# Delta-rule recurrence and top-1 experts on one core: products merged per head pair and per two batches, and expert tables read one expert ahead

## The chip, the core and the metric

The kernel runs on one core of a Trainium2 chip. A core has a matrix engine (TensorE; PE in the profile, its weight loads PEld), a vector engine (VectorE, DVE), a scalar engine (ScalarE, ACT), GpSimd (POOL), SyncE (SP), which here issues DMAs, and 16 DMA engines. Matrix products read their weights and their moving operand from SBUF and write into PSUM, which VectorE and ScalarE read. The metric is the device time of one execution in microseconds.

## The reference

Part one is a gated delta rule for 4 batches and 8 heads over 768 positions with heads of 48; part two sends each of the 3,072 rows to one of 8 experts (384 to 1,024 to 384).

```python
k_n = k / (norm(k) + 1e-6)
state = zeros(B, H, D, D)                       # B, H, S, D = 4, 8, 768, 48
for t in range(S):
    y[t]  = q[t] @ state
    v_old = k_n[t] @ state
    state = state + beta[t] * outer(k_n[t], v[t] - v_old)
x = y as (B*S, H*D)
logits = x @ w_gate
e = argmax(logits);  g = softmax(logits)[e]
out = g * (relu(x @ w1[e]) @ w2[e])             # per row, w1 384x1024, w2 1024x384
```

## The kernel before

**The recurrence in chunks.** The 768 positions are cut into 24 chunks of 32, and a block is four chunks. Partition 32b + s holds position s of a chunk of batch b. Within a chunk the rule is a triangular system: with G the products of keys with keys, u = inverse(I + scaled strict G) times (scaled v - k times state), then state += k'u and y = q times state + masked(q k')u. All products are fp32, and one fp32 matmul stands in the trace as two records of TensorE and two weight loads.

Heads go in pairs. Head 2p is on partitions 0 to 47 and head 2p + 1 on 64 to 111 of `kq_t` (keys and queries, transposed, by block), and the state `st_t` is [112, B, 4 pairs, 48] in the same way. TensorE is used in tiles: `tile_position` gives the row and column at which a small weight is put, so that small products of different tiles lie beside each other.

**One step t of the loop (one chunk), in TensorE's order:**
- `residual`, L288: key times state, 32 products with a 48 x 32 weight and 48 moving columns, into two PSUM tiles `ks`; VectorE subtracts each from v (L299, two instructions)
- `turn`, L360: three 128 x 128 transposes of the previous step's output row, for the logits; ScalarE copies them (L361, L362)
- `state_out`, L305: query times state, 32 products, into `yb`
- `dummy`, L467: 24 products of a row of zeros (bf16, 192 columns) into spare PSUM columns; nothing reads them
- `apply`, L316: the inverse `wt` times v, 32 products 32 x 32 by 48; ScalarE copies the result to `u` (L318, twice)
- `logits`, L368, of the previous step, and every second step the slots of the rows (L388 to L437; TensorE's part is L407 and L410)
- `update`, L328: keys times u, 32 products with 64 rows, into two PSUM tiles `S`; keys come from `kz_t`, which holds zeros where a row belongs to the other batch. ScalarE copies S to `st_t` (L332, twice)
- `inside`, L341: the masked query-key product `gk_t` times u, 32 products 32 x 32 by 48, into `yb`; ScalarE copies the row (L354)
- `gram`, L172, for the chunk nine ahead: keys times keys and queries, 32 products 48 x 32 by 64; ScalarE copies all of it to `gk_t` (L181), and VectorE masks the query part in SBUF one step before its use (L186, 256 elements a partition).

The order of every engine is written out by hand (`manual_schedule`). The inverse of the next block is a chain of 62 steps on VectorE (`lanes`, L259 and L266: multiply, subtract), with a square root on ScalarE at its front (L214) and transposes (L272); `beside(t, i)` puts `STEPS = (3, 3, 3, 2, 2, 2, 2)` of them, and as many slot operations, between the parts of step t. ScalarE also scales v (L281, eight instructions a step). Loads of `kq` for the block three ahead go out at t = 0, 4 and 8, on SP's queue. From t = 16 or so GpSimd and SP already fetch the first expert's rows, and from t = 20 its weights are split into a high and a low part (L473, L474).

**The experts.** Each has room for 448 rows. `find` (L508 to L518) reads a table `xi` of the rows' numbers from DRAM on SP's queue, `fetch` (L522) gathers the rows `xr` from DRAM with GpSimd, `tokens` transposes them on TensorE (L598 and L601 for the first expert, L791 and L792 later); `ffn` runs the two layers (L542, L552), each as three products of high and low parts, with `relu` on ScalarE and VectorE (L545, L546). While expert e runs its 12 places, `tokens` of expert e + 1 advances at the places in `TOK`, and the weights of e + 1 are loaded and split at those in `PC`.

**Before the loop** the first block's inverse runs on VectorE, nine Grams run on TensorE, and 16 and then 40 dummies stand among them.

Of the kernel before, what the change touches and what calls it, by code (L numbers as in the profile page):

```python
# [21 lines left out]
TB = 4  # L22
# [19 lines left out]
def deltanet_moe(ctx, tc, kq, kv, bl_in, w_gate, w1, w2, out):  # L42
# [14 lines left out]
    qmask = cp.tile([128, 32], F32, name="qmask")  # L57
# [25 lines left out]
    DU = 24  # L83
    TS = 5
    TOK = (0, 2, 6, 8, 9, 10)
    PC = (1, 3, 4, 6, 8, 9, 11)
    TOK0 = (0, 2, 6, 8, 9, 10)
# [18 lines left out]
    S_ = [pss.tile([128, 2, NP, D], F32, name=f"S{g}") for g in range(2)]  # L106
    ks_b = [pss.tile([128, 512], F32, name=f"ks{a}") for a in range(2)]
    ks_ = [x[:, 0:NP * D].rearrange("t (p e) -> t p e", p=NP) for x in ks_b]
    yb = pss.tile([128, 2, 512], F32, name="yb")
    y_ = yb[:, :, 0:NP * D].rearrange("t a (p e) -> t a p e", p=NP)  # L110
# [6 lines left out]
    gk_t = [home(j).tile([128, TB, H, 2, 32], F32, name=f"gk{j}") for j in range(4)]  # L117
    kz_t = [lp.tile([128, 2, DM], F32, name=f"kz{j}") for j in range(3)]
# [4 lines left out]
    st_t = lp.tile([128, B, NP, D], F32, name="st")  # L123
    tiles = {tb: {} for tb in range(NT)}

    def load_kq(tb, x, engs):
        for a in range(2):
            engs[a].dma_start(out=kq_t[tb % 4][64 * a:64 * a + D, x], in_=kq[tb, a, :, x])

    def load_kz(n):  # L130
        for b in range(B):
            r = slice(32 * b, 32 * b + 32)
            nc.sync.dma_start(out=kz_t[n % 3][r, b % 2], in_=kv[n, r, 0])

    def load_v(n):
        nc.sync.dma_start(out=v_t[n % 4].rearrange("p h d -> p (h d)"), in_=kv[n, :, 1])

    def constants():
# [3 lines left out]
                                pattern=[[1, 128]], channel_multiplier=-1)  # L142
        for b in range(B):
            r = slice(32 * b, 32 * b + 32)
            nc.gpsimd.tensor_copy(qmask[r], cmask[r, r])
# [15 lines left out]
    def kq_of(n, x, a, p, b):  # L161
        return kq_t[n // TB % 4][64 * a:64 * a + D, x, n % TB, p, b]

    def gram(n, psum, x0, x1):
        i = n % TB
        kt = kq_t[n // TB % 4]
        gv = psum[:, :, 0:256].rearrange("s a (p x t) -> s a p x t", p=NP, x=2)
# [9 lines left out]
    def gk_view(n, x0, x1):  # L177
        return gk_t[n // TB % 4][:, n % TB, :, x0:x1].rearrange("s (p a) x t -> s a p x t", a=2)
# [527 lines left out]
    for t in range(NN):  # L706
# [33 lines left out]
        if t + 1 < NN:  # L740
            mask_q(t + 1)
# [274 lines left out]
```

## Time and profile before

| | |
|---|---|
| time | 713.64 us, median of 3 runs (713.09 to 714.28) |
| the profiled execution | 716.45 us, its span 714.7 us |
| mean granted clock of TensorE | 0.849 of full speed |
| TensorE matmul records | 11,617, busy 550.7 us (77% of the span) |
| TensorE weight loads | 11,617, busy 495.9 us (69%) |
| VectorE | 1,273 instructions, 326.8 us (46%) |
| ScalarE | 626 instructions, 235.8 us (33%) |
| GpSimd | 132 instructions, 108.3 us (15%) |

The span is what the hardware profiler saw between the first and the last instruction; the 1.75 us by which the execution is longer lie around it. Busy times overlap between engines, and a matmul record's duration is longer than the distance to the next one where records are pipelined or run in different tiles, so the busy share of TensorE says little about how much of it could be saved. The granted clock has two levels in the records, 1.0 for 2.4 GHz and 0.5 for 1.2 GHz; a mean lies between them. An idle engine stands with what ended its wait; "issue" is time in which it waited for nothing that the profile shows.

### The profile page before, as it was taken

To read this page: it belongs to the slowest core of one execution; us is meant where nothing else is said; L and a number is where in the kernel's file an instruction comes from. 1 tells how busy PE (TensorE), PEld (TensorE's weight loads), DVE (VectorE), ACT (ScalarE), POOL (GpSimd) and SP (SyncE) were. 2 spreads that over 40 slices of the span, in tenths; PEclk is the share of its full clock that TensorE was granted. 3 is DMA by queue.
4 is the path that set the end of the run, shared out by engine and by line. 5 is a ranking of instruction groups with operands and counts; after the bars stand their busy time and mean duration, and the time that the engine had idled before them with its cause. 6 is when DMAs were issued, how large, how long until landed. Compare 5 with 4: busy or idle time off the path is not lost.

```text
span 714.7 us, 26302 instructions
## 1 busy us (share of the span) xinstructions
PE 550.7 (77%) x11617; PEld 495.9 (69%) x11617; DVE 326.8 (46%) x1273; ACT 235.8 (33%) x626; POOL 108.3 (15%) x132
## 2 busy tenths in 40 slices
PE   3253886586657767877877889799999999999991
PEld 3243775475556556766766789688988989898991
DVE  3937255364526366466443243363435363545311
ACT  1222232233224323333243243243434343434320
POOL 5000001010001101011012021331313222313111
PEclk9997787678768666779686789899999999999996
DMA  4867043605440530242234240463434353444000
GB/s 96 162 117 182 15 85 97 126 15 120 105 95 8 126 90 14 53 112 51 57 94 122 63 122 23 128 192 110 140 116 143 107 146 125 142 124 134 24 14 19
DMA packets 58037, 68.12 MB, mean 95 GB/s; under 512 B 30961, under 2 KB 50714, under 8 KB 56768
## 3 DMA queue, kind: packets, MB, share of 16 engines
q1 hardware_dynamic: 53056, 56.02, 31.2%
q0 software_dynamic: 4800, 10.00, 4.3%
q8 instruction: 91, 1.49, 1.0%
q10 hardware_dynamic: 64, 0.39, 0.2%
q14 instruction: 26, 0.21, 0.1%
HBM read 53.46 MB, written 13.02 MB: 93 GB/s over the span
## 4 chain that ended last, share of the span: by engine, by line
PE 57%; issue 19%; DMA 10%; ACT 6%; DVE 5%; POOL 2%; SPq 0%; POOLq 0%; DVEq 0%; ACTq 0%
PE y L552 12%; PE ks L467 11%; PE h L542 10%; DMA xr<-xn,xi 4%; PE gb L172 3%; PE S L328 3%; PE y L825 3%; PE ks L316 3%; ACT v L281 3%; PE yb L305 2%; PE ks L368 2%; PE yb L341 2%; DMA kq<-in_kq_dram 2%; PE ks L288 2%; DMA st_d<-idi,sli 2%
## 5 line engine op out<-in xcount | busy, mean ns | idle before, releaser
L467 PE MATMUL ks<-zrow 128*128 128x192 bf16 x608 | 92.4, 341 | 8.0 <-DVE v L299 6.1
L552 PE MATMUL y<-w2h,hx 128*128 128x384 f32 x352 | 96.2, 348 | 0.0
L467 PEld LDWEIGHTS <-zrow 128*128 128x128 bf16 x608 | 80.0, 137 | 16.2 <-issue 6.9
L444 POOL DMA_INDIRECT st_d<-idi,sli x24 | 25.9, 1080 | 361.4 <-DVE sli L437 225.3
L266 DVE TENSOR_TENSOR lw<-lw,tmp 128x84 f32<-128x84 f32 (+26 forms) x372 | 76.4, 248 | 0.0
L259 DVE TENSOR_TENSOR tmp<-lg,lw 128x84 f32<-128x84 f32 (+26 forms) x372 | 76.3, 247 | 0.0
L552 PEld LDWEIGHTS y<-w2h,hx 128*128 128x128 f32 x352 | 66.3, 195 | 0.9
L318 ACT COPY u<-ks 128x192 f32<-128x192 f32 x48 | 15.2, 318 | 150.7 <-PE ks L316 150.3
L172 PE MATMUL gb<-kq 48*32 48x64 f32 (+1 forms) x1664 | 27.5, 249 | 46.1 <-issue 28.8
L474 DVE TENSOR_TENSOR w2l<-w2r,w2h 128x768 fp32r<-128x768 f32 x32 | 30.9, 969 | 68.1 <-ACT w2h L473 67.8
L542 PE MATMUL h<-xl,w1h 128*128 128x448 f32 x168 | 61.6, 367 | 0.0
L542 PE MATMUL h<-xh,w1l 128*128 128x448 f32 x168 | 61.6, 367 | 0.0
L542 PE MATMUL h<-xh,w1h 128*128 128x448 f32 x168 | 61.4, 366 | 0.0
L552 PE MATMUL y<-w2l,hx 128*128 128x384 f32 x176 | 60.7, 345 | 0.0
L555 POOL DMA_INDIRECT out_dram<-yo,xi x32 | 31.4, 982 | 167.3 <-ACT yo L820 122.2
L172 PEld LDWEIGHTS gb<-kq 48*32 48x32 f32 x1664 | 21.3, 124 | 50.8 <-issue 36.1
L305 PE MATMUL yb<-st,kq 48*32 48x48 f32 x1472 | 24.6, 269 | 36.7 <-ACT xT L362 21.6
L305 PEld LDWEIGHTS yb<-st,kq 48*32 48x32 f32 x1472 | 19.3, 140 | 45.8 <-ACT xT L362 29.7
L522 POOL DMA_INDIRECT xr<-xn,xi x33 | 39.5, 1196 | 61.7 <-DMA xi<-st_d 54.4
L546 DVE SCALAR_TENSOR_TENSOR hx<-h,hx 128x448 fp32r<-128x448 f32 (+1 forms) x64 | 37.1, 584 | 22.9 <-ACT hx L545 22.5
L281 ACT ACTIVATE v<-v,nt_all 128x48 f32<-128x48 f32 x192 | 45.7, 325 | 0.0
L288 PE MATMUL ks<-st,kq 48*32 48x48 f32 x1472 | 29.7, 236 | 20.5 <-issue 18.0
(151 smaller groups left out, 925.2 us busy)
## 6 DMA issues: line engine op xcount, KB each, us to landing
w1r<-in_moe_w_dram SPq DMA_DIRECT2D x24, 512.0 KB
w2r<-in_moe_w_dram SPq DMA_DIRECT2D x32, 384.0 KB
kq<-in_kq_dram SPq DMA_DIRECT2D x23, 384.0 KB
v<-in_kv_dram SPq DMA_DIRECT2D x24, 192.0 KB
kz<-in_kv_dram SPq DMA_DIRECT2D x96, 48.0 KB
xn<-row SPq DMA_DIRECT2D x10, 394.0 KB
gd<-gk SPq DMA_DIRECT2D x20, 128.0 KB
lg<-gd SPq DMA_DIRECT2D x5, 512.0 KB
```

Source lines behind the costliest of these rows:

```text
L172: nc.tensor.matmul(gv[32 * b:32 * b + 32, a, p, x0:x1], lhsT=kt[r, 0, i, p, b], rhs=kt[r, x0:x1, i, p, b], start=True, stop=True, tile_pos ...
L259: nc.vector.tensor_tensor(out=x, in0=lg[:, r0:r1, c:c + 1].broadcast_to([128, r1 - r0, b - a]), in1=lw[:, c:c + 1, a:b].broadcast_to([128, ...
L266: nc.vector.tensor_tensor(out=lw[:, r0:r1, a:b], in0=lw[:, r0:r1, a:b], in1=x, op=ALU.subtract)
L281: nc.scalar.activation(out=vn[:, h], in_=vn[:, h], func=AF.Copy, scale=nt[:, h:h + 1])
L288: nc.tensor.matmul(dst[32 * b:32 * b + 32, p], lhsT=kq_of(n, x, a, p, b), rhs=st_t[64 * a:64 * a + D, b, p], start=(p == 0), stop=True, ti ...
L305: nc.tensor.matmul(y_[32 * b:32 * b + 32, a, p], lhsT=kq_of(n, 1, a, p, b), rhs=st_t[64 * a:64 * a + D, b, p], start=(p == 0), stop=True, ...
L467: nc.tensor.matmul(ks_b[1][:, 320:512], lhsT=busy[:, 0:128], rhs=busy[:, 0:192], start=True, stop=True, skip_group_check=True)
L522: nc.gpsimd.indirect_dma_start(out=XR[e][:, g], out_offset=None, in_=xn[0:128 * nt], in_offset=bass.IndirectOffsetOnAxis(ap=XI[e][:, g, 0: ...
L542: nc.tensor.matmul(ps, lhsT=w[:, d, fs], rhs=x_[:, d], start=(n == 0), stop=(n == len(terms) - 1))
L546: nc.vector.scalar_tensor_tensor(out=hl, in0=ps, scalar=0.0, in1=hh.bitcast(F32), op0=ALU.max, op1=ALU.subtract)
L552: nc.tensor.matmul(ps, lhsT=h(f)[h_], rhs=w2[w][:, f, :], start=(n == 0), stop=(n == len(terms) - 1))
L555: nc.gpsimd.indirect_dma_start(out=out, out_offset=bass.IndirectOffsetOnAxis(ap=idx, axis=0), in_=yo, in_offset=None, bounds_check=N - 1, ...
```

## The change

The order of the loop stays; most products get larger and fewer.

- **State per head pair.** `st_t` is block-diagonal, [112, B, 4, 96]: head 2p in rows 0 to 47 and columns 0 to 47, head 2p + 1 in rows 64 to 111 and columns 48 to 95, zeros elsewhere (set once, by GpSimd). `residual` and `state_out` are 16 products each, 112 x 32 by 96, into `kb` and `yb`, which hold 384 columns in a row. One subtraction and one copy of u, each of 384 elements, stand where two of 192 stood.
- **Update by batch rows.** Each batch has its own PSUM bank in `S`; 16 products use the 32 rows of one batch, 112 weight columns and 96 moving ones. `kn_t` is one load a chunk, padded to 112 columns per pair, in place of four into `kz_t`. Two ScalarE copies bring the diagonal blocks, 768 elements on 48 partitions each, into `st_t`.
- **Grams of two batches.** 16 products, 48 x 64 by 128, give the Grams of two batches with each other too. ScalarE copies the key part to `gk_t`; VectorE multiplies the query part with `qmask` (now 64 wide, zero outside each batch's own block) straight from PSUM into `gq_t` (12 buffers). The mask so stands with the Gram, nine chunks ahead of its use. `inside` is 16 products 64 x 64 by 48.
- **Dummies** are fp32, 128 x 128, and eight a step (`DU`) in place of 24; they stand before `state_out`. Before the loop they are 10 and 24 in place of 16 and 40.
- **`turn`** writes into `gb`, which the Gram leaves free, and is copied by one instruction.
- **Start.** The first block's key Grams are made by `gram0` into `gb`, and VectorE transposes them straight from PSUM. All nine Grams then follow, with five steps of the inverse between each Gram and its copy. A `kq` load covers 112 rows in one DMA.
- **Expert tables.** `find` runs one expert ahead: expert 1's table is read before expert 0's, from then on the table of e + 1 behind the gathers of e, with three buffers in place of two, and `TOK` has one place less.

```diff
-    DU = 24
+    DU = 8
...
-    TOK = (0, 2, 6, 8, 9, 10)
+    TOK = (0, 6, 8, 9, 10)
...
+    S_ = pss.tile([128, B, 512], F32, name="S")
+    sv = S_[:, :, 0:DM].rearrange("d b (p f) -> d b p f", p=NP)
+    kb = pss.tile([128, 512], F32, name="kb")
+    ks = kb[:, 0:DM]
+    yb = pss.tile([128, 512], F32, name="yb")
...
+    kn_t = [lp.tile([128, NP, 112], F32, name=f"kn{j}") for j in range(3)]
...
+    st_t = lp.tile([128, B, NP, 2 * D], F32, name="st")
...
+    def gram(n):
+        i, kt = n % TB, kq_t[n // TB % 4]
+        for p in range(NP):
+            for c in range(2):
+                for a in range(2):
+                    r, bs = slice(64 * a, 64 * a + D), slice(2 * c, 2 * c + 2)
+                    nc.tensor.matmul(gb[64 * c:64 * c + 64, a, 128 * p:128 * p + 128],
+                                     lhsT=kt[r, 0, i, p, bs].rearrange("d b t -> d (b t)"),
+                                     rhs=kt[r, :, i, p, bs].rearrange("d x b t -> d x (b t)"), start=True, stop=True,
+                                     tile_position=(64 * a, 64 * c), skip_group_check=True)
+
+    def gram_copy(n):
+        gv = gb.rearrange("s a (p x t) -> s p a x t", p=NP, x=2)
+        if n >= TB:
+            nc.scalar.copy(out=gk_t[n // TB % 2][:, n % TB].rearrange("s (p a) t -> s p a t", a=2), in_=gv[:, :, :, 0])
+        nc.vector.tensor_tensor(out=gq_t[n % GQ].rearrange("s (p a) t -> s p a t", a=2), in0=gv[:, :, :, 1],
+                                in1=qmask.unsqueeze(1).unsqueeze(1).broadcast_to([128, NP, 2, 64]), op=ALU.mult)
...
+    def from_state(x, n, dst):
         for p in range(NP):
             for b in range(B):
...
+                nc.tensor.matmul(dst[32 * b:32 * b + 32, 2 * D * p:2 * D * p + 2 * D], lhsT=kq_of(n, x, p, b),
+                                 rhs=st_t[0:112, b, p], start=(p == 0), stop=True, tile_position=(0, 32 * b),
+                                 skip_group_check=True)
...
     def residual(n):
...
+        from_state(0, n, kb)
+        nc.vector.tensor_tensor(out=vflat(n), in0=vflat(n), in1=ks, op=ALU.subtract)
...
+    def update(n):
+        kn, u = kn_t[n % 3], u_t[n % 2]
         for p in range(NP):
             for b in range(B):
...
+                r = slice(32 * b, 32 * b + 32)
+                nc.tensor.matmul(sv[0:112, b, p], lhsT=kn[r, p], rhs=u[r, 2 * p:2 * p + 2].rearrange("t a e -> t (a e)"),
+                                 start=(n == 0 and p == 0), stop=True, tile_position=(32 * b, 0), skip_group_check=True)
         for a in range(2):
...
+            r, c = slice(64 * a, 64 * a + D), slice(D * a, D * a + D)
+            nc.scalar.copy(out=st_t[r, :, :, c], in_=sv[r, :, :, c])
...
     def inside(n):
...
+        gq, u = gq_t[n % GQ], u_t[n % 2]
+        for h in range(H):
+            for c in range(2):
+                r = slice(64 * c, 64 * c + 64)
+                nc.tensor.matmul(yb[r, D * h:D * h + D], lhsT=gq[r, h], rhs=u[r, h], start=(n == 0 and h == 0), stop=True,
+                                 tile_position=(64 * c, 64 * c), skip_group_check=True)
...
     def dummy(k):
         for _ in range(k):
-            nc.tensor.matmul(ks_b[1][:, 320:512], lhsT=busy[:, 0:128], rhs=busy[:, 0:192], start=True, stop=True,
+            nc.tensor.matmul(yb[:, DM:512], lhsT=zrow[:, 0:128], rhs=zrow[:, 128:256], start=True, stop=True,
                              skip_group_check=True)
...
-            XI[e] = rp.tile([128, NG + 1, 2], I32, name=f"xi{e}", tag="xi", bufs=2)
+            XI[e] = rp.tile([128, NG + 1, 2], I32, name=f"xi{e}", tag="xi", bufs=3)
...
-    dummy(40)
+    dummy(24)
...
             turn(t - 1)
+            dummy(DU)
             state_out(t)
-            dummy(DU)
...
-            gv = gram(t + GA, gb, 0, 2)
-            gram_copy(t + GA, gv, 0, 2, nc.scalar.copy)
+            gram(t + GA)
+            gram_copy(t + GA)
...
-        if t + 1 < NN:
-            mask_q(t + 1)
...
     def tokens(e, X):
-        find(e, 0 if e > 0 else NG)
         if e == 0:
             X.extend(X0["x"])
-        yield
+            find(0, NG)
+            find(1)
+            yield
         fetch(e, 0 if e > 0 else NG)
+        if 0 < e < E - 1:
+            find(e + 1)
         yield
```

TensorE's order in a step of the loop, from `inside` to the dummies, before (numbers behind a name tell buffers apart; 24 pairs of the last two rows follow each other):

```order
L341 MATMUL yb<-u_130,gk_118 32x48 x32
L172 MATMUL gb<-kq_116 32x64 x32
L288 MATMUL ks_110<-st,kq_114 32x48 x16
L288 MATMUL ks_111<-st,kq_114 32x48 x16
L360 MATMUL yb<-ident,row_1013 128x128 x3
L305 MATMUL yb<-st,kq_114 32x48 x32
L467 LDWEIGHTS zrow
L467 MATMUL ks_111<-zrow 128x192
```

and after, up to the logits:

```order
L331 MATMUL yb<-u_138,gq_121 64x48 x16
L179 MATMUL gb<-kq_115 64x128 x16
L292 MATMUL kb<-st,kq_113 32x96 x16
L349 MATMUL gb<-ident,row_1618 128x128 x3
L455 MATMUL yb<-zrow 128x128 x8
L292 MATMUL yb<-st,kq_113 32x96 x16
L311 MATMUL kb<-v_135,wt_1469 32x48 x32
L356 MATMUL kb<-wg,xT_140 128x8 x3
```

Four groups of 32 products are now 16 (`inside` L331, Gram L179, residual and state_out L292), the eight dummies stand ahead of state_out, and the transposes L349 write into the Gram's tile `gb`.

VectorE's order with its semaphore waits, from a mask to the next subtraction, before (`lg`, `lw` and `tmp` belong to the inverse, 128 x n is the size):

```order
L186 TENSOR_TENSOR gk_118<-gk_118,qmask 128x8x32
L266 TENSOR_TENSOR lw_173<-lw_173,tmp_2_1018 128x14x3 [waits DVE_49]
L266 TENSOR_TENSOR lw_173<-lw_173,tmp_2_1018 128x15x3 [waits DVE_49]
...
L259 TENSOR_TENSOR tmp_5_1084<-lg_654,lw_173 128x78 [waits DVE_49]
L259 TENSOR_TENSOR tmp_5_1084<-lg_654,lw_173 128x78
L299 TENSOR_TENSOR v_126<-v_126,ks_110 128x4x48 [waits DMAHW6_49,PE_49,Activation_49]
L299 TENSOR_TENSOR v_126<-v_126,ks_111 128x4x48 [waits PE_49,Activation_49]
```

and after:

```order
L188 TENSOR_TENSOR gq_126<-gb,qmask 128x512 [waits Activation_49]
L263 TENSOR_TENSOR tmp_11_1024<-lg_615,lw_181 128x120 [waits DVE_49]
L263 TENSOR_TENSOR tmp_11_1024<-lg_615,lw_181 128x120
L270 TENSOR_TENSOR lw_181<-lw_181,tmp_11_1024 128x10x12 [waits DVE_49] x2
...
L270 TENSOR_TENSOR lw_181<-lw_181,tmp_13_1044 128x18x12 [waits DVE_49]
L270 TENSOR_TENSOR lw_181<-lw_181,tmp_13_1044 128x18x2 [waits DVE_49]
L301 TENSOR_TENSOR v_135<-v_135,kb 128x384 [waits DMAHW4_49,PE_49]
```

The mask stood at the same place and waited for no other engine; it now reads `gb` and waits for ScalarE, whose Gram copy comes just before it, and the inverse's steps and the subtraction stand behind it.

SP's queue at the last table reads ahead of the expert loop, before:

```order
L516 DMA xi_6810<-st_d 64x2 x2
L513 DMA xi_7991<-st_d 128x4
L518 DMA xi_7991<-st_d 128x2
L516 DMA xi_7991<-st_d 64x2 x2
L488 DMA w2r_0_8013<-in_moe_w_dram 128x2x384
```

and after:

```order
L504 DMA xi_4701<-st_d 64x2 x2
L501 DMA xi_5578<-st_d 128x4
L506 DMA xi_5578<-st_d 128x2
L504 DMA xi_5578<-st_d 64x2 x2
L501 DMA xi_5598<-st_d 128x4
L506 DMA xi_5598<-st_d 128x2
L504 DMA xi_5598<-st_d 64x2 x2
L476 DMA w2r_0_5620<-in_moe_w_dram 128x2x384
```

A second table, expert 2's, is read at the same place, ahead of a load of expert weights. GpSimd's order has not changed.

## Rows read from the trace of the kernel before

**Rows 1.** The page: busy time and share of the span of each engine with its instructions, and one row of its DMA queues (packets, MB, share of 16 engines).

```profile
PE 550.7 (77%) x11617; PEld 495.9 (69%) x11617; DVE 326.8 (46%) x1273; ACT 235.8 (33%) x626; POOL 108.3 (15%) x132
...
q8 instruction: 91, 1.49, 1.0%
```

**Rows 2.** Busy times of the loop and of the experts. Columns: start and end in us, length, busy us (and records) of PE, PEld, DVE, ACT and POOL, granted clock, DMA share, GB/s.

```profile
58.00:400.00 342.00, 246.61 (x8863) 213.97 (x8863) 169.80 (x885) 109.70 (x387) 24.03 (x23) 0.74 0.34 80
485.00:715.00 230.00, 209.30 (x1116) 197.16 (x1115) 91.83 (x150) 83.45 (x140) 52.52 (x54) 0.97 0.34 103
```

**Rows 3.** The chain of waits that ended last, in order of time: start in us, us, engine, what, line, records.

```profile
58.02 2.12 PE S L328 x44
...
189.64 1.43 PE ks L316 x64
...
253.70 4.00 PE ks L467 x24
...
384.03 1.15 PE S L328 x53
...
503.25 11.05 PE h L542 x54
```

**Rows 4.** What the engines waited for from 58 to 400 us, TensorE and VectorE: the waiting group, what ended the wait, total us, times, longest.

```profile
PE ks L288 <- issue: 18.0, 10, 2.9
PE gb L172 <- issue: 17.3, 8, 4.2
...
PE yb L305 <- issue: 15.0, 5, 5.4
...
PE S L328 <- issue: 5.3, 2, 3.7
...
DVE r L216 <- ACT s L214: 17.4, 5, 5.5
```

**Rows 5.** The DMA queues from 58 to 345 us, the row of TensorE's instructions.

```profile
q8 instruction: 58, 0.95, 1.6%
```

**Rows 6.** The timeline of some places: start in us, us, engine, line, what, tile, shapes, and in brackets the idle time before with what ended it.

```profile
239.38 0.88 PE L316 MATMUL ks<-v,wt 32*32 32x48 f32 x64
...
241.54 1.14 PE L328 MATMUL S<-u,kz 64*64 64x48 f32 x64
...
242.78 0.86 ACT L332 COPY st<-S 112x384 f32<-112x384 f32 x2 [0.96 <-PE S L328]
...
246.51 0.68 PE L172 MATMUL gb<-kq 48*32 48x64 f32 x32 [2.63 <-issue]
...
398.54 1.14 PE L328 MATMUL S<-u,kz 64*64 64x48 f32 x64
...
415.61 0.50 PE L542 MATMUL h<-xe,w1h 128*128 128x256 f32 x2 [0.70 <-DVE xe L474]
...
438.64 1.45 PE L598 MATMUL xt<-one,row 128*128 128x64 f32 x12
...
440.02 0.88 PE L601 MATMUL xt<-ident,xr 64*128 64x64 f32 x6
```

**Rows 7.** The table of Rows 2 for two applies.

```profile
189.70:191.00 1.30, 1.30 (x64) 1.19 (x63) 0.00 (x0) 0.32 (x1) 0.00 (x0) 0.50 0.00 0
239.40:240.20 0.80, 0.80 (x65) 0.73 (x65) 0.00 (x0) 0.21 (x1) 0.00 (x0) 1.00 0.93 373
```

**Rows 8.** Groups by line over the whole span: line, engine, operation, out<-in, shapes, count, busy us, mean ns of one, idle time before and what ended it.

```profile
L316 PE MATMUL ks<-v,wt 32*32 32x48 f32 x1536 | 25.3, 222 | 2.3 <-issue 2.3
...
L332 ACT COPY st<-S 112x384 f32<-112x384 f32 x46 | 19.7, 481 | 25.7 <-PE S L328 25.7
...
L318 ACT COPY u<-ks 128x192 f32<-128x192 f32 x48 | 15.2, 318 | 150.7 <-PE ks L316 150.3
...
L299 DVE TENSOR_TENSOR v<-v,ks 128x192 f32<-128x192 f32 x46 | 15.2, 351 | 27.0 <-PE ks L288 16.4 <-issue 10.4
...
L186 DVE TENSOR_TENSOR gk<-gk,qmask 128x256 f32<-128x256 f32 x24 | 10.0, 418 | 0.0
...
L546 DVE SCALAR_TENSOR_TENSOR hx<-h,hx 128x448 fp32r<-128x448 f32 (+1 forms) x64 | 37.1, 584 | 22.9 <-ACT hx L545 22.5
...
L427 DVE TENSOR_TENSOR pos<-pos,ohb 128x16 f32<-128x16 f32 (+1 forms) x14 | 2.4, 172 | 0.4
...
L542 PEld LDWEIGHTS h<-xh,w1h 128*128 128x128 f32 x168 | 31.6, 188 | 2.6
```

**Rows 9.** The timeline of VectorE in the first inverse: its first operation, the first of its 62 steps, and the transpose at its end.

```profile
14.50 0.19 DVE L210 TENSOR_SCALAR ss<-lg 128x32 f32<-128x32 f32 x1
...
18.47 0.25 DVE L259 TENSOR_TENSOR tmp<-lg,lw 128x15 f32<-128x15 f32 x2
...
39.28 1.96 DVE L272 STREAM_TRANSPOSE wt<-lw 128x1024 f32<-128x1024 f32 x1
```

**Rows 10.** Waits for gathered rows and their tables: TensorE from 470 us on, and GpSimd over the whole span.

```profile
PE xt L792 <- DMA xr<-xn,xi: 5.9, 6, 1.3
...
PE xt L791 <- DMA xr<-xn,xi: 1.7, 2, 1.3
...
POOL xr L522 <- DMA xi<-st_d: 54.4, 9, 9.6
```

More of the change, by code (lines that the diff above doesn't have):

```diff
@@ L301, in state_out, with apply @@
     def state_out(n):
+        from_state(1, n, yb)
+    def apply(n):
+        wt, vn, u = tiles[n // TB]["wt"], v_t[n % 4], u_t[n % 2]
+        for h in range(H):
+            for b in range(B):
+                r = slice(32 * b, 32 * b + 32)
+                nc.tensor.matmul(kb[r, D * h:D * h + D], lhsT=wt[r, n % TB * H + h], rhs=vn[r, h],
+                                 start=True, stop=True, tile_position=(32 * b, 32 * b), skip_group_check=True)
+        nc.scalar.copy(out=u.rearrange("t h e -> t (h e)"), in_=ks)
@@ L320, in update @@
-    def update(n):
-        kz, u = kz_t[n % 3], u_t[n % 2]
-        for s in range(2):
-            for p in range(NP):
-                for g in range(2):
-                    r = slice(64 * g, 64 * g + 64)
-                    for a in range(2):
-                        h, m = 2 * p + a, 64 if a == 0 else D
-                        nc.tensor.matmul(S_[g][64 * a:64 * a + m, s, p], lhsT=kz[r, s, h * D:h * D + m], rhs=u[r, h],
-                                         start=(n == 0 and s + p == 0), stop=True, tile_position=(64 * g, 64 * a),
-                                         skip_group_check=True)
-        for g in range(2):
-            nc.scalar.copy(out=st_t[0:112, 2 * g:2 * g + 2], in_=S_[g][0:112])
@@ L334, in inside @@
[L334 to L343 removed]
+                r = slice(32 * b, 32 * b + 32)
@@ L651, in deltanet_moe @@
     scale_v(1)
-    for n in range(TB, GA):
-        gv = gram(n, gb, 0, 2)
-        gram_copy(n, gv, 0, 2, nc.scalar.copy)
-        if n % TB == TB - 1:
+    for n in range(GA):
+        gram(n)
+        run(lane, 5)
+        gram_copy(n)
+        if n % TB == TB - 1 and n >= TB:
             grams_out(n // TB)
-    run(lane, 30)
-    mask_q(0)
-    run(lane, 20)
+    run(lane, 5)
     lw = tiles[0]["lw"]
-    nc.tensor.matmul(ks_b[1][0:32, 320:321], lhsT=lw[:, 10, 0:32], rhs=lw[:, 10, 0:1], start=True, stop=True,
+    nc.tensor.matmul(yb[0:32, DM:DM + 1], lhsT=lw[:, 10, 0:32], rhs=lw[:, 10, 0:1], start=True, stop=True,
                      skip_group_check=True)
-    dummy(40)
+    dummy(24)
     run(lane, 100)
@@ L843, in deltanet_moe @@
         for t in range(KF + NG + 1):
[L844 removed]
+            if e == 0 and t in (0, TS):
                 run(tok0)
```

154 lines of the change are left out of this document (52 added, 102 removed).

## The prediction, made before the changed kernel ran

> **What bounds the kernel now.** I read the stage table first. The recurrence, 58 to 400 us, takes 342 of the 714.7 us, the experts from 485 us on 230 [rows 2]. The chain of waits then gives the step: S L328, the state update, starts at 58.02 and, 21 updates later, at 384.03 [rows 3], 326.0 / 21 = 15.5 us a step. TensorE has 246.6 us of records there at a mean granted clock of 0.74, VectorE 169.8 us [rows 2]; neither fills the stretch. The waits say why: TensorE waits for "issue", 18.0 + 17.3 + 15.0 + 5.3 = 55.6 us in four rows [rows 4], and the timeline has one such wait inside a Gram, 2.63 us in front of its second half [rows 6]. The page gives the cause: TensorE's records are 11,617 matmuls and 11,617 weight loads, and queue q8 "instruction" carries 91 packets and 1.49 MB [rows 1]. That is 64 B a record and 256 records a packet. In this stretch TensorE executes 2 x 8,863 records [rows 2], 17,726 / 22 = 806 a step or 3.1 packets, and from 58 to 345 us 58 packets arrive [rows 5], one in 4.9 us. So the step is limited largely by how fast TensorE gets its instructions, and in part by a clock that is at 1.2 GHz half the time.
>
> **TensorE, part by part.** The 32 products of apply are 64 records in 0.88 us at a granted clock of 1.00 (2.4 GHz) and in 1.43 us at 0.50 (1.2 GHz) [rows 3, 6, 7]. Less the 0.22 us of the last record [rows 8], and with 16 records in each of its four tiles, that is 41 and 76 ns a record: about two cycles for each of 48 columns. Weight loads behave alike: 12 records with 128 weight columns and 64 moving ones take 440.02 - 438.64 = 1.38 us [rows 6], 115 ns each, again two cycles per column. So I price a product at (records per tile) x 2 x (the larger of moving and weight columns), tiles side by side, at full clock. Residual and state_out, four tiles: 8 x 192 cycles, 0.65 us each. Update, four tiles: 8 x 224, 0.8. Inside, two tiles: 16 x 128, 0.9. Gram, four tiles: 8 x 256, 0.9. Eight fp32 dummies: 16 x 115 ns, 1.85, where 24 bf16 ones took up to 4.00 [rows 3]. Apply, transposes and logits stay, 0.7, 0.4 and 0.7. No shape of the new tiles is in the trace. The lower bound for the new products is apply's 0.66 us / 63, 10.5 ns a record, or 0.35 us for 32; the upper one is that their tiles take turns (among the rivals). I take the tile price, since the 64x64 update of now, 1.14 us at full clock [rows 6], fits it: 16 records of 128 cycles are 0.85, plus the end of the last one.
>
> Records per step: 4 for each of 112 products (16 + 16 + 32 + 16 + 16 + 16), 6 for transposes, 12 for logits, 32 for dummies, about 4 for slots: 502 against 806, 2.0 packets instead of 3.1. At 4.9 us a packet that asks for 9.6 us a step.
>
> **The chain of a step after it.** ScalarE copies grow from 318 ns at 192 elements a partition to 481 at 384 [rows 8]: 0.85 ns an element. The state copies become two of 768 elements, 0.8 each, 1.5 us for both (now 0.86 [rows 6]; bounds 1.3 and 2.0). The mask now reads the Gram in PSUM, 512 elements: 0.67 us by the 584 ns of a PSUM operation of 448 [rows 8], with bounds of 0.42 (256 from SBUF) and 0.75. One subtraction of 384 takes 0.55 in place of two of 0.35 [rows 8].
>
> The mask is the new wait. What it waits for, the Gram copy, stands in ScalarE's order behind the state and row copies. Behind it on VectorE stand six steps of the inverse and the next subtraction, and the next step's transposes on TensorE wait for it too. From the end of an update: state copies until 1.6 us, row copy 2.05, Gram copy 2.65, mask 3.35, then six inverse steps of 0.33 (the first inverse: 39.28 - 18.47 less 0.42, over 62 steps [rows 9]) and some four slot operations of 0.17 [rows 8] until 6.0, subtraction 6.6, apply 7.5, u copy 8.05, update 9.05, with hand-overs 9.3. TensorE's own path (residual 1.8 to 2.7, transposes after the mask 3.8, dummies 5.7, state_out 6.4) lies just inside. VectorE's sum is nearly as long: one inverse, from its first operation at 14.50 to the end of its transpose at 41.24, is 26.3 us without the mask in it [rows 9], 6.6 a step over four steps; with subtraction 0.55, mask 0.67 and six slot operations a step, 8.8 us. On top comes ScalarE's square root, for which VectorE waits 17.4 / 5 = 3.5 us per inverse [rows 4], 0.8 us a step, and 0.1 for short packet waits: **10.2 us a step**. It is 9.3 if these hide, and 11.3 if short waits on both engines add up.
>
> Three steps load two blocks of kq, and TensorE's packets queue behind those loads; I keep 5 us for each, 15 in all, worked out from nothing better than the longest issue waits now.
>
> **The other stages.** Start to the first update, 58.0 us [rows 3]: the second kq load now starts behind a transpose of about 1.96 us [rows 9] and carries 112 rows instead of 96, and VectorE puts nine masks of 0.67 between the steps of the first inverse, where it had one of 0.42. The 24 fp32 dummies are 48 records, 5.5 us at full and 11 at half clock; they run beside the end of that inverse. Against it stand fewer Gram records (544 matmul records for 832) and eight small loads that became two. I come to 58 again, plus or minus 4. From the last update to the first early expert matmul, 398.54 to 415.61, 17.1 us [rows 6], there is one step and some hand-overs: 13. From there it is 299.1 us to the end, experts mostly. TensorE waits 5.9 + 1.7 = 7.6 us for xr in it, and GpSimd's gathers wait 54.4 us for tables [rows 10] that are now read one expert ahead. With the microseconds at half clock that follow the longest of these waits I take 9.5 (0 if another wait takes its place, 12 at most). No queue gains work there: on SP's queue the table reads move ahead of an expert's weight loads.
>
> **Sum**, against the profiled execution of 716.45 us: 1.75 around the span + 58 + 22 x 10.2 + 15 + 13 + 289.6 = 601.75. In general it is 377.4 + 22 P for a step of P us. The median of the runs shown, 713.64, lies 2.8 lower, so I predict **599 us**.
>
> **Rivals.** *Half clock* (0.14). At 1.2 GHz the step's products are 14.5 us of TensorE: residual and state_out 1.3 each, transposes 0.7, dummies 3.5, apply and logits 1.3 each, update, inside and Gram 1.7 each. For it: two applies, each right behind a burst of dummies, have 0.50 and 1.00 [rows 7], and the dummies become half as long. Against it: the idle stretches between bursts now are those of missing instructions. A step of 15 us half the time gives P = 12.2 and 646 - 2.8 = 643.
> *Instructions still bind* (0.10). The same data arrive in two thirds of the time, so a packet may need 6 us instead of 4.9: P = 11.8, 634.
> *The inverse hides better* (0.08). Mask and inverse steps overlap the rest: P = 9.0, 573.
> *Tiles take turns* (0.04), the slower side. Residual and state_out now use all rows and differ only in columns. If tiles that share rows work one after the other, each of 32 records costs 80 ns of stream and 27 of weights, 3.4 us instead of 0.65, and a Gram 16 records of 160 ns, 2.6: P about 16, 729 - 2.8 = 726. It decides from P = 15.4 on, where 377.4 + 22 P reaches 716.45. Against it: 54 expert matmuls, all on the same rows, take 11.05 us [rows 3], 205 ns each, while one load takes 188 ns [rows 8] and 448 columns at 2.4 GHz 187: load and stream overlap there.
> [...]
> That *the table read gains nothing* moves the sum by 9.5 us only and lies inside the range.
>
> **How the numbers follow.** The forecast (P from 9.3 to 11.3, 579 to 623) has 0.64. The range reaches to the half-clock case and to the one of 9.0 with a shorter start: 565 to 645. About 0.2% is what a measurement of this kernel can tell from no change; only the tiles' case and a hundredth of unknowns reach there: faster 0.95, same 0.01, slower 0.04.
>
> **What would show it.** About 63 instruction packets (502 records a step) and issue waits of TensorE under 25 us between first and last update; S starts some 10.2 us apart; the mask's wait for the Gram copy among VectorE's largest, and the subtraction on the chain; a granted clock over 0.9 there; residual near 0.65 + 0.2 us (2.6 or more would be the tiles' case); no wait for xr on TensorE from the third expert on. I am wrong if update starts lie over 12 us apart, or if the start grows by more than 6 us.

## The result and the profile after

The changed kernel takes 629.38 us (median of 4 runs, 620.08 to 632.35) against 713.96 of the kernel before: a ratio of 0.874, 95% interval 0.864 to 0.884. The ratio compares the means of the runs that lie within 1.5% of the fastest of their kernel (625.1 and 715.4 us), the others counting as slow; the two medians would give 0.882. The forecast was 599 us, with a range of 565 to 645. The profiled execution took 620.08 us with a span of 618.3.

The page of the changed kernel, its busy times and the queue that carries TensorE's instructions, as in [rows 1]:

```profile
PE 523.7 (85%) x7701; PEld 480.2 (78%) x7701; DVE 331.0 (54%) x1248; ACT 247.3 (40%) x572; POOL 102.0 (17%) x131
...
q8 instruction: 61, 1.00, 0.7%
```

Its table by stage, with the columns of [rows 2]: from the first update of the state to the last, from there to the first early expert matmul, and the rest.

```profile
55.74:309.69 253.95, 209.98 (x5297) 188.37 (x5297) 168.02 (x848) 120.78 (x340) 22.95 (x23) 0.89 0.42 114
309.69:327.68 17.99, 12.09 (x261) 10.42 (x260) 7.02 (x27) 7.42 (x17) 3.53 (x3) 0.85 0.30 77
327.68:618.28 290.60, 268.64 (x1468) 252.67 (x1468) 121.39 (x221) 110.07 (x190) 65.51 (x69) 0.95 0.35 109
```

The loop's 22 intervals now take 253.95 us, 11.5 each, where they took 340.5 [rows 3, 6]; the rest from the first early expert matmul went from 299.1 to 290.6 us. So 86.6 of the 96.4 us between the two profiled executions lie in the loop and 8.5 in the experts. TensorE's records there are 2 x 5,297 / 22 = 482 an interval. At a clock of 0.74 [rows 2] about 178 us of the loop stood at half clock before, at 0.89 about 56 us do now. How the 86.6 us divide between records, clock and waits, no run tells.

The two levels in the trace of the kernel before, by its dummies: those at 253.70 in [rows 3] took 4.00 us at a clock of 0.50, and at 1.00

```profile
336.34 2.14 PE ks L467 x24
```

So they follow each other, 192 columns each, in 158 and 82 ns, or 1.2 and 2.3 columns a nanosecond. The 1.2 and 2.4 GHz of the prediction stand for these two levels.

What the engines waited for from first to last update, as in [rows 4]:

```profile
PE gb L349 <- DVE gq L188: 8.5, 12, 1.0
PE kb L356 <- ACT u L313: 7.7, 13, 0.6
PE kb L311 <- DVE v L301: 6.4, 4, 2.0
PE kb L395 <- ACT u L313: 5.4, 9, 0.6
PE kb L356 <- DVE base L403: 4.8, 9, 0.5
PE kb L395 <- DVE ohb L390: 3.9, 1, 3.9
...
PE yb L331 <- issue: 1.4, 2, 1.0
```

```profile
DVE gq L188 <- ACT gk L187: 36.6, 15, 4.4
DVE w1l L462 <- ACT w1h L461: 13.2, 3, 9.7
```

The waits for "issue", 55.6 us of TensorE in [rows 4], are 1.4 us. A longer single wait that [rows 4] leaves out went with them, that of state_out for ScalarE's copy of the transposes:

```profile
PE yb L305 <- ACT xT L362: 21.0, 22, 1.9
```

The transposes wrote into `yb`, the tile of state_out; with `turn` in `gb` that wait is gone. The prediction has no term for it. What is left are short waits, for the mask (L349 are the transposes), for the copy of u (L356 are the logits, L395 the slots) and, four times, for the subtraction in front of apply (L311).

One step at full clock in the timeline of the changed kernel, from one update to the next; the columns are those of [rows 6]:

```profile
162.80 1.04 PE L320 MATMUL S<-u,kn 32*112 32x96 f32 x32
...
163.97 1.61 ACT L324 COPY st<-S 48x768 f32<-48x768 f32 x2 [0.89 <-PE S L320]
...
164.74 1.05 PE L179 MATMUL gb<-kq 48*64 48x128 f32 x30
...
165.73 0.87 PE L292 MATMUL kb<-st,kq 112*32 112x96 f32 x32
165.98 0.59 ACT L187 COPY gk<-gb 128x512 f32<-128x512 f32 x1
...
166.60 0.69 DVE L188 TENSOR_TENSOR gq<-gb,qmask 128x512 f32<-128x512 f32 x1 [2.02 <-ACT gk L187]
...
167.35 0.55 PE L349 MATMUL gb<-ident,row 128*128 128x128 f32 x3 [0.75 <-DVE gq L188]
...
167.73 1.95 PE L455 MATMUL yb<-zrow 128*128 128x128 f32 x16
...
169.61 0.87 PE L292 MATMUL yb<-st,kq 112*32 112x96 f32 x32
...
169.69 0.55 DVE L301 TENSOR_TENSOR v<-v,kb 128x384 f32<-128x384 f32 x1
...
170.41 0.88 PE L311 MATMUL kb<-v,wt 32*32 32x48 f32 x64
...
171.36 0.48 ACT L313 COPY u<-kb 128x384 f32<-128x384 f32 x1 [2.63 <-PE kb L311]
...
171.89 0.83 PE L356 MATMUL kb<-wg,xT 128*128 128x8 f32 x6 [0.60 <-ACT u L313]
...
172.66 1.04 PE L320 MATMUL S<-u,kn 32*112 32x96 f32 x32
```

The reader is to see that the step of 9.86 us follows TensorE's order: it stands for 0.75 us in front of the transposes, until Gram copy and mask are through, and 0.60 us in front of the logits, until u is copied, and else it works but for short gaps. The subtraction ends at 170.24 and apply starts at 170.41, when state_out is through: VectorE comes in just in time. With slot products in the step it is 10.84 us. Steps that lie partly at a clock of 0.50 take 11 to 14.

### The profile page after: what moved, and what is told of

Same layout as the page of the kernel before. It is cut to its first block, busy times and chain, and to the rows that moved or that the text cites. A ratio compares the mean times of both kernels' runs of the same rounds, so it can differ in the third digit from the quotient of the medians.

```text
span 618.3 us, 18249 instructions
## 1 busy us (share of the span) xinstructions
PE 523.7 (85%) x7701; PEld 480.2 (78%) x7701; DVE 331.0 (54%) x1248; ACT 247.3 (40%) x572; POOL 102.0 (17%) x131
## 4 chain that ended last, share of the span: by engine, by line
PE 66%; ACT 9%; DVE 9%; issue 7%; DMA 5%; POOL 1%; SPq 0%; POOLq 0%; ACTq 0%; DVEq 0%
PE h L530 17%; PE y L540 15%; PE yb L455 5%; PE gb L179 5%; PE S L320 4%; PE y L809 4%; ACT st L324 3%; PE kb L311 3%; PE kb L356 3%; PE yb L331 3%; DVE gq L188 2%; PE yb L292 2%; DMA kq<-in_kq_dram 2%; ACT u L313 2%; PE kb L292 2%
## 5 line engine op out<-in xcount | busy, mean ns | idle before, releaser
L540 PE MATMUL y<-w2h,hx 128*128 128x384 f32 x352 | 94.9, 344 | 0.0
L462 DVE TENSOR_TENSOR w2l<-w2r,w2h 128x768 fp32r<-128x768 f32 x32 | 30.9, 969 | 79.2 <-ACT w2h L461 78.6
L455 PE MATMUL yb<-zrow 128*128 128x128 f32 x436 | 61.7, 304 | 1.4 <-DVE warm L602 1.4
L455 PEld LDWEIGHTS yb<-zrow 128*128 128x128 f32 x436 | 60.1, 222 | 1.4 <-DVE warm L602 1.4
L179 PE MATMUL gb<-kq 48*64 48x128 f32 x768 | 41.3, 367 | 16.6 <-DVE gq L188 9.0
L533 ACT ACTIVATE hx<-h 128x448 fp32r<-128x448 f32 (+1 forms) x64 | 33.0, 517 | 45.7 <-PE h L530 45.7
L179 PEld LDWEIGHTS gb<-kq 48*64 48x64 f32 x768 | 33.1, 189 | 19.9 <-DVE gq L188 12.2
L324 ACT COPY st<-S 48x768 f32<-48x768 f32 x46 | 36.5, 793 | 23.6 <-PE S L320 23.0
L804 ACT ACTIVATE yo<-y,gt 128x384 f32<-128x384 f32 x22 | 12.8, 581 | 77.6 <-PE y L540 63.0
L313 ACT COPY u<-kb 128x384 f32<-128x384 f32 x24 | 11.5, 478 | 74.6 <-PE kb L311 64.7
L188 DVE TENSOR_TENSOR gq<-gb,qmask 128x512 f32<-128x512 f32 x24 | 16.6, 691 | 45.3 <-ACT gk L187 40.4
```

Source lines behind the costliest of these rows:

```text
L179: nc.tensor.matmul(gb[64 * c:64 * c + 64, a, 128 * p:128 * p + 128], lhsT=kt[r, 0, i, p, bs].rearrange("d b t -> d (b t)"), rhs=kt[r, :, i ...
L324: nc.scalar.copy(out=st_t[r, :, :, c], in_=sv[r, :, :, c])
L455: nc.tensor.matmul(yb[:, DM:512], lhsT=zrow[:, 0:128], rhs=zrow[:, 128:256], start=True, stop=True, skip_group_check=True)
L462: nc.vector.tensor_tensor(out=lo, in0=src, in1=hi.bitcast(F32), op=ALU.subtract)
L533: nc.scalar.activation(out=hh, in_=ps, func=AF.Relu)
L540: nc.tensor.matmul(ps, lhsT=h(f)[h_], rhs=w2[w][:, f, :], start=(n == 0), stop=(n == len(terms) - 1))
```

## The experiments

**The same kernel again, and records added.** The first run repeats the changed kernel for a second trace; the second puts tiny products behind the dummies:

```diff
             dummy(DU)
+            tiny(SM)            # SM = 152: bf16, weight 32 x 32, 8 columns, tiles in turn
```

> The changed kernel once more, for its spread and a second trace. Its times so far are 620.1 to 632.4 us. If the spread comes from the stretches at half clock in the loop, a trace with a longer time has more of them (57.8 us between first and last update in the first trace, where the loop took 253.9 us), while steps at full clock stay at 9.9 us, or 10.8 with slot products. If it comes from elsewhere (loads, experts), the loop is 254 us again and the difference lies behind 328 us.

> The changed kernel with 152 tiny products a step more (bf16, 32 x 32 by 8, four tiles, results not read), 304 records, so that a step has about 806 records as before the change. Theory of the prediction (delivery of TensorE's instructions limited the loop): about 3.1 packets a step at 4.9 us, steps of 15 us, TensorE's waits for issue back at 40 us or more in the loop, time about 700 us. Rival (work, not the number of records, set the step): only the products' own time is added, about 1 to 2 us a step, waits for issue stay under 15 us in the loop, time 645 to 665 us.

The repeat took 626.98 us (623.2 to 631.9); its profiled execution, 631.9 us, has the loop so:

```profile
55.40:322.04 266.64, 223.86 (x5296) 200.60 (x5296) 168.11 (x848) 121.12 (x340) 22.82 (x23) 0.82 0.39 109
```

The kernel before took 708.61 us beside it, a ratio of 0.885 (0.880 to 0.890). Against the first trace the loop is 12.7 us longer and the whole execution 11.8 us, so the difference between these two lies in the loop, where the clock is 0.82 for 0.89. With the two levels of 0.50 and 1.00, a stretch of length T at mean clock c has 2 (1 - c) T at half clock: 96 us against 56. Forty more microseconds at half clock go with 12.7 us of time, about 0.3 us each, and the 56 of the first trace are worth some 18 us. A step at full clock is 9.85 us again. Not all of the 12.7 need be the clock's: TensorE's waits for issue are 4.3 us here (2.6 in front of L331, 1.7 in front of L311).

With the added records the time is **737.31 us** (ratio 1.039 to the kernel before, 1.032 to 1.046), 110 us above the repeat. Its loop and its longest waits of TensorE there:

```profile
55.70:423.56 367.86, 297.64 (x8640) 268.99 (x8640) 168.40 (x848) 121.89 (x340) 22.83 (x23) 0.72 0.29 80
```

```profile
PE kb L312 <- issue: 18.6, 11, 2.8
PE yb L293 <- issue: 16.2, 7, 4.0
...
PE yb L458 <- issue: 5.5, 4, 1.6
```

```profile
L458 PE MATMUL yb<-zrow 32*32 32x8 bf16 x3344 | 30.8, 168 | 5.5 <-issue 5.5
```

The tiny products themselves are busy 30.8 us (L458), 1.4 a step. With 785 records a step the waits for issue are back at 41 us (these three and 0.7 more), the clock falls to 0.72, and the step is 16.7 us, longer than before the change. The rival, 645 to 665 us, falls: records with next to no arithmetic bring back the step of the kernel before, its waits and its clock. How the 110 us divide between missing instructions and the clock, beyond the 31 of work, the run doesn't tell, nor whether the clock fell behind the waits or behind the tiny products themselves.

That such waits are for instructions can be read in the traces of the two kernels. TensorE's 23,234 matmuls and weight loads before the change came in 91 packets of q8 [rows 1], 255 a packet. Counted in order by 256, all 29 waits for issue behind the first update in the loop before end within seven records of each other (179 to 185), and 1.2 to 1.7 us after a packet has come (the one in front of that update does not, at record 117 and 5.8 us); so do the two of the changed kernel, at 185 and 183, 1.4 and 1.5 us after one.

**Dummies.** `DU = 8` became 0 and 16.

> The changed kernel without the eight dummies of a step (nothing that is read is left out). Theory (in a step at full clock the dummies fill a gap in which TensorE would wait for VectorE's subtraction): such steps stay within 0.3 us of 9.9 and 10.8 us, the subtraction becomes the longest wait in front of apply (about 1.9 us each), and stretches at half clock grow from 57.8 us of the loop to 90 us or more: 625 to 650 us. Rival (the dummies lie on the path): steps at full clock shorten by 1.5 us or more, and the time falls below 610 us.

> The changed kernel with 16 dummies a step in place of eight. Theory (eight just fill the gap): a step at full clock grows by 1.7 to 1.9 us, 22 steps 40 us, and at most the 20 us that half clock costs now come back: 635 to 665 us, granted clock in the loop over 0.95. Rival (the clock is worth more than the gap): the time falls by 5 us or more, below 622 us.

Without dummies 625.98 us, the same as the repeat; with sixteen 652.86. Their loops:

```profile
55.25:316.92 261.67, 205.16 (x4944) 176.41 (x4944) 167.94 (x848) 121.82 (x340) 22.84 (x23) 0.72 0.40 110
```

```profile
56.80:343.08 286.28, 247.23 (x5648) 225.95 (x5648) 168.40 (x848) 120.68 (x340) 23.05 (x23) 0.90 0.36 101
```

And the waits for the subtraction without dummies:

```profile
PE kb L311 <- DVE v L301: 23.5, 16, 3.8
```

Sixteen go nearly as the theory had it: a first step of 11.64 us (updates at 56.83 and 68.47) is 1.8 more than with eight, 40 us in 22 steps, and the time is 26 us above the repeat. The clock is 0.90, about that of the first trace (0.89) and not the 0.95 expected. Without dummies both statements are half right: the first step at full clock is 8.85 us (updates at 55.26 and 64.11), so eight dummies do lengthen the path, by 1.0 of their 1.9 us; most of the rest is now waited for at the subtraction (0.72 us in this step). But half clock grows to 2 x 0.28 x 261.7 = 147 us, and the two cancel.

**Four suspects of a step.** The logits in another PSUM tile, `yb`; more of the inverse ahead of the mask; the mask ahead of the Gram copy (the two statements of `gram_copy` exchanged); and the tables read late again (`find(e)` in its old place, two buffers).

```diff
-        ps = kb[:, DM + E * (n % 2):DM + E * (n % 2) + E]
+        ps = yb[:, DM + E * (n % 2):DM + E * (n % 2) + E]
...
-            nc.tensor.matmul(yb[:, DM:512], lhsT=zrow[:, 0:128], rhs=zrow[:, 128:256], start=True, stop=True,
+            nc.tensor.matmul(yb[:, DM + 16:512], lhsT=zrow[:, 0:128], rhs=zrow[:, 128:240], start=True, stop=True,
```

```diff
-        inverses(STEPS[i], t)
+        inverses(ISTEPS[i], t)          # ISTEPS = (4, 4, 4, 4, 1, 0, 0)
```

> The changed kernel with the logits written to another PSUM bank (yb in place of kb, 16 columns that the dummies leave free), so that they need not wait until ScalarE has copied u out of kb. Theory (the logits' wait of 0.6 us stands on the path between apply and update in each step, and my sum left it and the 0.8 us of the logits out): steps at full clock become 9.2 to 9.4 us in place of 9.85, and 10.2 to 10.4 with slots in place of 10.84, loop 10 to 13 us shorter, time 612 to 618 us. Rival (VectorE has to finish an inverse in four steps, so what a step saves is waited for at the end of a block): ordinary steps shorten, but TensorE's waits for the subtraction grow from 5 to 10 us or more in the loop and the time stays at 622 to 630 us.

> The changed kernel with VectorE's steps of the inverse dealt out as 4, 4, 4, 4, 1, 0, 0 in place of 3, 3, 3, 2, 2, 2, 2: four more of them ahead of the mask, where VectorE waits for the Gram copy, and four fewer between the mask and the subtraction. Theory (that wait of 1.5 to 2 us a step is lost to the inverse, so that the subtraction stands late at the end of each block, TensorE idles 1.9 us there and the clock falls behind it): the waits of apply for VectorE at 97, 147 and 193 us go, DVE's waits for the Gram copy fall from 36.6 us to under 20 us, half clock in the loop falls under 45 us, time 605 to 618 us. Rival (the mask comes later in the steps with slots and holds up TensorE's transposes): TensorE's waits in front of the transposes grow from 8.5 us to 15 us or more, the time stays or rises, 625 to 640 us.

> The changed kernel with VectorE's mask ahead of ScalarE's Gram copy. Theory (TensorE's own path sets a step; the transposes wait for whoever reads the Gram last): mask and copy still follow each other, a step at full clock changes by no more than 0.3 us (9.85 to 9.6 at best), time 620 to 630 us. Rival (the mask's wait for the Gram copy is the new wait that sets the step, as the prediction had it): the mask starts 0.9 us earlier, steps at full clock become 9.0 to 9.2 us, time 605 to 613 us.

> The changed kernel with the expert tables read as before the change (one place ahead of their gathers, two buffers). Theory (7.6 us of waits for gathered rows and what half clock follows them): from the first early expert matmul to the end 298 to 300 us in place of 290.6, GpSimd waits 39 us or more for tables again, time 633 to 637 us. Rival (another wait stood behind them): 290 to 292 us from there on, time 622 to 629 us.

These four ran where the kernel before took 709.04 us, beside the repeat 708.61.

*Logits.* In this first form the first product of the logits carries the start flag in `yb`, between state_out and inside. By the author's reading the part of the output that comes from the state is so left out, and the rows go to other experts. It took 762.18 us, with TensorE waiting 143.4 us behind the experts for a gather that the other runs don't have, so only its loop is read: steps at full clock of 9.17 and 10.13 us, as the theory had it.

*The inverse earlier* gave 624.02 us, within the spread. VectorE's wait for the Gram copy fell from 36.6 to 32.6 us only, and neither the waits for the subtraction (4.2 us) nor the clock (0.86) changed as expected. The transposes waited 7.3 us, not more than before, so the rival falls too. Alone it does nothing that can be measured.

*The mask first* gave 627.71 us. A step at full clock stayed at 9.85 us (updates at 55.46 and 65.31) and one with slots went from 10.84 to 10.51 (updates at 78.50 and 89.01). Now the Gram copy waits for the mask, and the transposes for the copy, as long as before:

```profile
59.36 0.59 ACT L189 COPY gk<-gb 128x512 f32<-128x512 f32 x1 [0.63 <-DVE gq L186]
60.00 0.55 PE L349 MATMUL gb<-ident,row 128*128 128x128 f32 x3 [0.75 <-ACT gk L189]
```

So their order matters little. The run does not take the wait for the two away, and the 0.75 us stay on TensorE's path in either order.

*The tables late* gave 636.86 us, 9.9 above the repeat. From the first early expert matmul to the end:

```profile
335.22:633.80 298.58, 270.72 (x1468) 252.44 (x1468) 120.63 (x221) 108.57 (x190) 70.21 (x69) 0.96 0.34 106
```

```profile
POOL xr L510 <- DMA xi<-st_d: 32.6, 6, 7.0
```

298.6 for 290.6 us, and GpSimd waits 32.6 us for tables in this stretch (39 or more were expected), where no such wait is left in the changed kernel. TensorE waits 11.4 us for gathered rows in it, for 5.8.

**The logits again, and combined.** The same tile, now added without a start flag (`start=False`); then together with the inverse's steps as above and a block's two `kq` loads one step apart; then this with four dummies and with none.

```diff
-        if t % TB == 0 and 3 <= t // TB + 3 < NT:
-            for x in range(2):
-                load_kq(t // TB + 3, x, nc.sync)
+        if t % TB < 2 and t // TB + 3 < NT:
+            load_kq(t // TB + 3, t % TB, nc.sync)
```

> The logits in yb once more, now added without a start flag, so that the sum of the output in that bank is kept. Theory (the logits' wait of 0.6 us stood on TensorE's path in each step, and the stretch with this wait, the slots' wait of 0.5 us and products of 8 columns is where the clock fell): steps at full clock 9.2 us and 10.1 with slots, half clock between first and last update under 45 us (57.8 and 81 us in the two traces of the changed kernel), time 608 to 618 us. Rival (what is saved is given back as waits for VectorE at the end of a block and for instructions): steps at full clock shorten as well, but the time stays at 621 to 630 us.

> Logits in yb, the inverse's steps dealt out as 4, 4, 4, 4, 1, 0, 0, and a block's load of queries one step after that of its keys, in place of both at once. Theory (waits of the loop add up: logits, end of a block, instructions behind the kq loads): gaps for instructions under 6 us in the loop where logits in yb alone had 12.7, waits of apply for VectorE under 4 us, loop under 240 us, time 600 to 612 us. Rival (the gaps for instructions don't come from the kq loads): they stay at 10 us or more and the time within 5 us of logits_bank_2.

> The same as combined_8 with four dummies a step. Theory (at eight, TensorE's path sets the step, and without the logits' wait the clock needs fewer dummies): steps at full clock 0.5 to 0.9 us shorter, half clock no more than 15 us longer, time 3 to 10 us below combined_8. Rival (as without dummies, what the path gains the clock takes): half clock 25 us or more longer than in combined_8, time equal to it or above.

> The same as combined_4 without any dummies in the steps (nothing that is read is left out). Theory (VectorE's chain to the subtraction takes over, as in the run without dummies, where a first step took 8.9 us at full clock): ordinary steps at full clock stay within 0.5 us of 8.4 us, TensorE's waits for the subtraction rise from 4 to 15 us or more, half clock grows by 25 us or more, time 588 to 605 us. Rival (the clock no longer needs dummies once the logits' wait is gone): half clock within 15 us of combined_4, time 578 to 585 us.

| run | time, us | loop, us | clock in the loop |
|---|---|---|---|
| changed kernel, repeated | 626.98 (623.2 to 631.9) | 266.6 (253.9 in the first trace) | 0.82 (0.89) |
| logits in yb | 609.11 (604.5 to 616.5) | 241.8 | 0.89 |
| combined, 8 dummies | 596.09 (593.7 to 599.9) | 230.7 | 0.93 |
| combined, 4 dummies | 585.27 (579.9 to 589.9) | 215.5 | 0.91 |
| combined, no dummies | 587.82 (584.3 to 593.3) | 227.5 | 0.81 |

The logits in yb, where a step at full clock looks so behind state_out, with no wait in front of L356:

```profile
164.79 0.88 PE L311 MATMUL kb<-v,wt 32*32 32x48 f32 x64
165.60 0.84 PE L356 MATMUL yb<-wg,xT 128*128 128x8 f32 x6
166.37 1.04 PE L320 MATMUL S<-u,kn 32*112 32x96 f32 x32
```

It is 17.9 us faster, with a step of 9.17 us (updates at 157.20 and 166.37). 22 steps of 0.68 are 15 us, nearly all of it; the clock, 0.89 and so 53 us at half, did not reach the 45 that I expected. The combination wins 13 us more, 4 us beyond the range expected. Its waits for issue are 4.8 us and those for the subtraction 4.4, where the logits alone left 5.3 and 8.0. So by the 0.3 us from above the clock, 0.93 and 32 us at half for 53, seems to have the larger part. Which of its two other edits did it was not tried apart; the waits for issue hardly fell, so the loads of kq are not shown to matter. Four dummies win 10.8 us more, with steps at full clock of 8.5 us (updates at 64.12 and 72.62): there the stretch at half clock hardly grew (39 us for 32). What TensorE waits for most is then Gram copy and mask, 16.9 us in front of the transposes. Without any dummies half clock does grow, to 86 us, TensorE waits 12.4 us for the subtraction, and a first step takes 7.74 us. The last row was taken on another chip, where the kernel before took 715.68 us; for the three rows above it took 708.19. So the last two rows are compared by their ratios to it: 0.824 (0.818 to 0.830) with four dummies and 0.820 (0.814 to 0.826) with none, which cannot be told apart. With four the kernel is 42 us below the repeat.

## Why the prediction was right, and where its size was off

**Instructions: right.** 61 packets came where about 63 were forecast, 482 records a step for 502, and waits for issue of 1.4 us for under 25. Adding the records back made the loop slower than it ever was, and the waits for issue keep to the packets. The rival that instructions still bind at 6 us a packet falls too: at 256 records in 6.1 us (482 in 11.5) TensorE waits 1.4 us in the whole loop. The 15 us for loads of kq in front of TensorE's packets were too many: the waits for issue are 1.4 and 4.3 us in all in the two traces. In the trace of the kernel before, the packets around these loads (issued from 58.6, 123.7 and 191.6 us on) came 8.4 to 9.9 us apart, five times, and all others of the loop 7.6 or less.

**Prices of TensorE: right.** Residual took 0.87 us (0.65 + 0.22 forecast), update 1.04 (0.8 + 0.22), dummies 1.95 (1.85). Tiles that share rows did not take turns in residual: that rival needed 2.6 us or more for it, and it took these 0.87. ScalarE's two state copies took 1.61 us (1.5) and the mask 0.69 (0.67).

**The step: nearly the right number by a wrong chain.** "Subtraction 6.6, apply 7.5, u copy 8.05, update 9.05" goes from the copy of u straight to the update. The logits, 0.83 us, and their wait of 0.60 for that copy stand between. (The prediction prices the logits, at 0.7, but not on this chain.) Up to the mask the chain held: it ended 3.45 us after the update, for 3.35. The logits write other columns of the tile kb than the copy reads, and in yb their wait went. The slots' product (L395), which doesn't read u and still writes kb in that run, went on waiting for the copy, 5.4 us in nine waits. Whether a product waits because of the tile or because of the PSUM bank, the runs do not tell. Behind the mask TensorE's own path, which I had "just inside", so became the one that sets the step, at 9.86 us, and 10.84 with slots; the subtraction is through 0.17 us before apply. I then added 0.9 us for ScalarE's square root and short packet waits, which don't set it; the two errors nearly cancel, 10.2 against a mean of 10.35 of these two kinds of step. The run without that wait (9.17 us) shows that the logits stood on the path.

**The clock: the term that was missing.** "A granted clock over 0.9" was 0.89 and 0.82. I gave the half-clock rival 0.14 and the forecast no microsecond at half clock in the loop; there were 56 and 96, some 18 us in the first trace by the repeat's ratio, an estimate from two traces. The ten falls in the loop of the first trace stand in the timeline behind one of two places: behind TensorE's wait for the subtraction at the end of a block (three), and behind the stretch from apply to the update with slots (five), in which TensorE waits 0.6 and 0.5 us between products of 8 to 16 columns; two more follow waits of 3 us and more in the last steps. One of either kind, with the columns of [rows 2]:

```profile
268.79:270.40 1.61, 1.08 (x14) 0.97 (x13) 1.20 (x10) 0.00 (x0) 0.00 (x0) 1.00 0.43 122
271.20:278.05 6.85, 6.85 (x88) 6.39 (x81) 3.51 (x12) 4.35 (x12) 1.96 (x2) 0.50 0.38 44
97.20:107.40 10.20, 9.61 (x199) 8.56 (x194) 4.93 (x27) 4.29 (x11) 0.00 (x0) 0.50 0.89 246
95.10:97.07 1.97, 0.00 (x1) 0.00 (x1) 1.97 (x4) 0.00 (x0) 0.69 (x1) 1.00 0.01 1
```

At 95.10 TensorE stood for 1.97 us while VectorE made the block's transpose and the subtraction behind it; from 97.20 the clock was 0.50. Not every such stretch is followed by a fall, so what decides is open.

**The end of the loop and the rest.** The last two of the 22 intervals took 13.75 and 14.39 us, 7.7 more than the 10.2 that I gave them all, and last update to first expert matmul 18.0 for 13. TensorE waits there for VectorE's slots, up to 3.9 us (L395 for L390), and VectorE, in whose order the slots stand behind that split's second half, waits 13.2 us for ScalarE's split of the first expert's weights (L462 for L461). The trace of the kernel before had this wait too:

```profile
389.39 0.17 PE L407 MATMUL ks<-ohb,ltri 128*128 128x8 bf16 x1 [3.48 <-DVE ohb L402]
```

Its reader is to see 3.48 us in front of the slots' product, in the last interval between updates. I had given that interval the length of all others, and the tail one step and hand-overs. The start, 55.7 us for 58, and the experts, 290.6 for 289.6, came as priced, and the tables' 9.5 us were 8.5, of which the run with the tables late shows 8.0.

**The sum.** Against the profiled execution: start -2.3, loop +14.6 (253.95 for 22 x 10.2 + 15), tail +5.0, experts and the edge +1.0 make +18.3, from 601.75 to 620.1. The other 12 us to the median are the step from one execution to the median: I took 2.8 off, as before the change, and the profiled execution turned out 9.3 us below it; the repeat suggests that this is a matter of how much of the loop lies at half clock. So of the 30 us by which the forecast was short, the half clock, taken as nothing, is by these estimates the largest term.

## What to carry to other kernels

Where an engine waits for "issue" and its instruction queue carries a packet every few microseconds (4.9 here), see whether the waits recur at the same record of a packet, and count records per step before arithmetic: merging products can then be worth more than their time (here 152 tiny ones a step, 30.8 us of work, came with 110 us). When such waits go, follow the whole order of the engine behind them, with every small product between the producer and the consumer of the chain; here a product and a copy that share one PSUM tile put 0.6 us a step there. And give the clock a term of its own where the new path still has short waits between thin products (here 0.89 and 0.82 in the loop, where over 0.9 was forecast).

## What the runs showed of the hardware that I had not expected

Eight fp32 dummies a step and none gave the same time (626.98 and 625.98 us), because a full-clock step shorter by 1.0 us was paid for by 147 us at half clock. With one wait less on the path four of them were better than eight by 10.8 us, and none was as good as four by the ratios. The changed kernel's times spread over 2% (620 to 632 us), though steps at full clock are equal to 0.01 us in the two traces (9.85 and 10.84). The traces part after the first interval, 10.99 against 14.29 us for the second, and at a clock of 1.00 against 0.76. In it TensorE waits for instructions, 1.0 us in the first trace and 2.4 in the repeat, so the parting seems to begin with a late packet and not with the clock. That a fall in one step then moves the next ones is a reading of two traces, not a test.
